# A two-stage attention with a squared-ReLU layer: five transposed blocks instead of six, keys in token order, and a new written-out order

## The chip, the cores and the metric

The kernel runs on one core of one Trainium2 chip. The metric is the device time of one execution in microseconds (us); less is better. The core has five engines with a stream of instructions each: TensorE (PE, matrix products; its weight loads are listed as PEld), VectorE (DVE), ScalarE (ACT), GpSimd (POOL) and SyncE (SP). Transfers are issued from the streams of SP, ACT and POOL.

## What is computed

```
q, k, v: (8, 8, 576, 64)      p: (8, 8, 32, 64)      # batch, head, token, channel; float32
def sm_attn(qq, kk, vv):
    s = 0.125 * (qq @ kk.T)
    s = s - max(s, axis=-1)
    a = exp(s);  a = a / (sum(a, axis=-1) + 1e-09)
    return a @ vv
packed = sm_attn(p, k, v)                 # 32 rows for each batch and head
x = sm_attn(q, packed, packed)            # 576 rows for each batch and head
x = x as (8 * 576 tokens, 8 * 64 channels)
out = (maximum(x @ w_in, 0) ** 2) @ w_out # 512 -> 2048 -> 512; out (4608, 512) float32
```

So 32 learned rows per head first gather the 576 tokens (the first softmax, over 576), and each token then reads these 32 rows (the second softmax, over 32).

## The kernel before

Four heads of one batch make a quad, whose 4 x 32 rows of p fill the 128 partitions; a batch has two quads. A token of a head is numbered l * 18 + t, with l from 0 to 31 (T = 18): l lies on the partitions of k and q after loading, t and the channel in the free dimension. VectorE transposes 32 x 32 blocks of 4-byte pairs, which puts channel pairs on the partitions. The matmuls are in bfloat16.

For a quad the steps are these, with the word of each in the order:

- `Lk`, `Lv` (load1, L284) and `Lq` or `LA`, `LB` (load_q, L268; for batches 0 and 1 in an A part of 320 tokens of each head and a B part of 256) load and cast, on POOL's queue. k of the first quad comes over SP and is cast by `kc`.
- `kT` (st_k, L341): VectorE turns the keys. The result's columns are in the order (j, l, a) with t = 6a + j, so each j from 0 to 5 owns 96 columns next to each other, and writes go in steps of 12 bytes.
- `s1` (st_s1, L371), `m1` (st_max1, L391), `x1` (st_exp1, L395): scores of the first softmax, maximum, exponential with sum, giving e1.
- `eT` (st_e1T, L409): PE transposes e1 in six blocks of 96 columns into a PSUM bank; `eo` (L415) copies it out. `pv` (st_pv, L425): for each block and head one small matmul with v, whose tile v_b holds six tokens on each of 96 partitions (J = 6, PS = 96), in a pool of three.
- `pp`, `bd`, `bs`, `pt`, `po`: scaling, the turned copies for the second scores, a copy with the partition halves exchanged (`bs`, L460), and the transposed copy ppT.
- `w0`, `w1` (st_wp, L540; for batch 0 `wa`, `wb`, `w1`) multiply ppT by w_in, so that the first layer follows from the second softmax alone; `W0`, `W1` (L551) copy wp out.
- `qT`, `s2`, `t2`, `m2`, `sb`, `x2`, `su`, `a2`, `aT`: the second softmax, with tokens on the partitions, and its turned result a2T (st_a2T, L531). For batches 0 and 1 each exists for the A and for the B part (`qA`, `zA`, `tA`, `mA`, `sA`, `xA`, `uA`, `aA`, `TA`, and with B).

For each batch, half of its tokens and block fb of 128 hidden channels (16 of them), `h` (step_h, L574) multiplies wp by a2T, `r` (L580) takes the ReLU, and `q` with numbers (step_q, L598) squares two blocks into gT, a ring of four batches. `o` (step_o, L609) adds two of the 16 hidden blocks for a tile of 128 output rows, `c` (step_c, L621) copies the tile out of PSUM and `d` (step_d, L630) sends it: two transfers on SP, each of 64 rows; for the last tile four, two on ACT's queue and two on SP's, of half the columns, after ACT and VectorE have each copied a half into the same tile.

The order of all this is written out by hand as one string of words, ORDER (L47). A suffix `:v`, `:a` or `:p` names the engine of a step where there is a choice. Each engine runs its instructions in the string's order and waits where data or a buffer is not there. `Z` with a number runs so many filler matmuls on PE (busy, L324), which keep PE going until the first real work. `pg` (p_next, L224) loads p of batch 1, `Pr`, `Px`, `Pt`, `Pu` (p_rest, L233) load, scale and turn p of the later batches; `Pu` makes pT1, the copy with the partition halves exchanged. `Wi` and `Wo` load w_in and w_out.

Of the kernel before, what the change touches and what calls it, by code (L numbers as in the profile page):

```python
# [20 lines left out]
P = 128  # L21
D = 64
NP = 32
J = 6
T = 18
PS = 96
S = J * PS
HALF = S // 2
QH = 4
SCALE = 0.125  # L30

# [20 lines left out]
h0.0.3 h0.0.9 r0.0.2:a Wo2 h0.0.8 aB01:v h0.0.10 r0.0.3:a TB00 r0.0.9:v r0.0.8:a h0.0.1 TB01 h0.0.11 q0.0.4:a  # L52
r0.0.10:v h0.1.2 q0.0.1:p r0.0.1:v h0.1.8 r0.0.11:a r0.1.2:v h0.1.1 q0.0.0:a r0.1.8:v h0.1.9 h0.1.0 r0.1.9:a LA1
q0.0.5:v w101 r0.1.1:a w100 q0.1.4:v W101:a h0.1.10 W100:v h0.1.3 h0.1.11 LB1 r0.1.0:a r0.1.3:a kT10 q0.1.0:p h0.0.12
r0.1.10:a r0.1.11:a h0.1.7 h0.1.14 q0.1.1:a r0.0.12:v h0.0.13 Wo1 r0.1.14:a kT11 h0.1.12 r0.1.7:a h0.0.4 q0.1.5:a
h0.1.5 Wo3 r0.0.13:v r0.1.12:a s11 q0.0.6:v r0.0.4:a Pr h0.0.5 r0.1.5:a m110 h0.0.6 r0.0.5:a h0.1.13 h0.1.6 r0.0.6:a
m111 h0.0.7 r0.1.13:a h0.1.4 x110 r0.0.7:v h0.1.15 r0.1.6:v h0.0.15 x111 r0.1.4:v eT10 q0.1.3:v h0.0.14 r0.1.15:v
q0.1.6:a o2.0 eo10:v q0.1.2:a eT11 q0.1.7:v o0.0 q0.0.3:a rd1 eo11:v o2.1 r0.0.14:a r0.0.15:v pv1 q0.0.2:a o0.1 pp1
o3.0 q0.0.7:a pt1 o1.0 bd1 o3.1 po1:v o1.1 Lv20 w110 w010 W110:v o3.2 o2.2 W010:a Lk21 o1.2 qA11 o0.2 qA10 w111 zA1
qB10 qB11 o2.3 W111:a tA11 o1.3 tA10 o3.3 mA11 o0.3 mA10 zB1 w011 sA11 o1.4 W011:a tB10 o0.4 tB11 sA10 o3.4 xA11 mB11  # L60
o1.5 xA10 mB10 o3.5 uA11 o0.5 uA10 o2.4 sB11 o0.6 aA11 o1.6 xB11 aA10 o2.5 Px Lv21 uB11 o0.7 TA11 Lv30 o1.7 TA10 c0:a
Pt o2.6 Lk20 c1:a d0 h1.0.0 aB11 o2.7 sB10 r1.0.0:a h1.0.1 TB11 c2:v h1.0.2 r1.0.1:a Pu o3.6 xB10 q1.0.0:v h1.0.4
r1.0.2:a o3.7 uB10 Lk31 r1.0.4:a o4.0 d2 kT21 c3:a h1.0.3 h1.0.12 r1.0.3:a aB10 o6.0 r1.0.12:a d1 q1.0.1:v h1.0.7
h1.0.5 r1.0.7:v o4.1 r1.0.5:a TB10 Lk30 h1.0.6 d3 q1.0.2:v h1.0.8 r1.0.6:a o6.1 r1.0.8:v q1.0.3:a h1.0.11 o6.2 h1.0.10
r1.0.11:v o4.2 kT20 Lq2 r1.0.10:a h1.0.9 o6.3 q1.0.5:a r1.0.9:v h1.0.14 s12 r1.0.14:v h1.0.15 q1.0.4:a m120 o4.3
h1.0.13 m121 o6.4 r1.0.15:a Lk40 x120 o4.4 q1.0.7:v o6.5 r1.0.13:v x121 o4.5 kT31 eT20 h1.1.10 rd2 q1.0.6:v eo20:a
eT21 r1.1.10:v h1.1.0 o6.6 eo21:v r1.1.0:a h1.1.6 kT30 h1.1.1 o4.6 Lk41 r1.1.6:a pv2 r1.1.1:v o6.7 pp2 h1.1.7 q1.1.0:v
c6:a h1.1.8 bd2 pt2 r1.1.7:v o4.7 r1.1.8:a bs2:v po2:a h1.1.5 c4:a h1.1.3 d6 q1.1.3:v w021 r1.1.5:a w020 r1.1.3:v o5.0
W020:a qT20 d4 h1.1.2 h1.1.11 Lk50 o7.0 qT21 r1.1.2:a W021:a o5.1 r1.1.11:v h1.1.13 o5.2 q1.1.1:v q1.1.5:a s22 Lv31
r1.1.13:v h1.1.4 o5.3 t220 r1.1.4:a h1.1.14 h1.1.9 Lv40 t221 o5.4 r1.1.9:a q1.1.2:a w120 Lq3 m220 w121 r1.1.14:a o5.5  # L70
W120:a m221 h1.1.12 o5.6 sb20:v W121:a h1.1.15 o5.7 sb21:v o7.1 r1.1.15:a c5:v x220 s13 Lq4 o7.2 q1.1.7:v q1.1.4:a
m130 o8.0 x221 d5 o7.3 su20 r1.1.12:a o8.1 o7.4 x130 su21 o8.2 q1.1.6:a o7.5 a220 o8.3 eT30 a221 o8.4 aT20 o7.6 eo30:a
aT21 o8.5 m131 h2.0.0 h2.0.1 r2.0.0:a o7.7 kT40 r2.0.1:a h2.0.2 x131 o8.6 c7:v Lk51 h2.0.3 r2.0.2:a o8.7 q2.0.0
r2.0.3:a qT30 h2.0.4 c8:a h2.0.7 d7 o9.0 rd3 r2.0.4:a q2.0.1 o10.0 qT31 r2.0.7:a h2.0.5 d8 eT31 kT41 r2.0.5:a Lq5
h2.0.6 eo31:a o9.1 r2.0.6:v h2.0.8 o10.1 q2.0.2 r2.0.8:a q2.0.3 h2.0.13 Lk60 h2.0.9 r2.0.13:v pv3 o9.2 pp3 r2.0.9:a
h2.0.10 h2.0.11 Lv41 q2.0.4 r2.0.10:a o9.3 r2.0.11:a bd3 pt3 h2.0.12 Lv51 bs3:v o9.4 po3:a r2.0.12:v h2.1.1 q2.0.5 s23
r2.1.1:a q2.0.6 h2.0.14 qT41 h2.1.2 r2.0.14:a o9.5 r2.1.2:a t231 h2.0.15 o10.2 r2.0.15:a qT40 h2.1.6 h2.1.0 r2.1.6:a
o9.6 q2.0.7 Lq6 h2.1.7 r2.1.0:a m231 o9.7 r2.1.7:a h2.1.3 q2.1.0 c9:a h2.1.4 q2.1.3 o10.3 r2.1.3:a sb31:v o11.0 d9
o10.4 r2.1.4:a t230 x231 h2.1.9 h2.1.5 q2.1.1 w130 su31 r2.1.5:a w030 r2.1.9:a o10.5 W030:a m230 h2.1.13 h2.1.10 o10.6
r2.1.13:a a231 r2.1.10:a o11.1 W130:a q2.1.2 h2.1.14 h2.1.11 sb30:v o11.2 r2.1.14:a o10.7 aT31 r2.1.11:a h2.1.12 x230  # L80
q2.1.5 h2.1.8 o11.3 c10:v r2.1.12:a r2.1.8:a w131 su30 w031 d10 o12.0 W031:a h2.1.15 q2.1.4 o12.1 q2.1.6 r2.1.15:a
a230 o11.4 W131:a o12.2 q2.1.7 o11.5 aT30 o12.3 h3.0.0 h3.0.2 o12.4 r3.0.0:v r3.0.2:a s14 h3.0.5 kT50 h3.0.4 r3.0.5:a
o11.6 m141 h3.0.1 Lk61 r3.0.4:a o12.5 r3.0.1:a kT51 h3.0.3 o11.7 x141 h3.0.12 r3.0.3:v o12.6 q3.0.0 r3.0.12:a h3.0.7
c11:a q3.0.2 h3.0.8 Lk70 q3.0.1 o12.7 r3.0.7:a m140 o13.0 d11 c12:a h3.0.13 r3.0.8:v o13.1 x140 r3.0.13:v h3.0.10
o14.0 d12 q3.0.6 r3.0.10:a h3.1.5 rd4 o13.2 r3.1.5:v h3.0.6 eT41 r3.0.6:v h3.0.11 o14.1 q3.0.3 r3.0.11:a h3.0.9 eo41:v
h3.1.0 eT40 r3.0.9:v o13.3 q3.0.5 r3.1.0:a o14.2 eo40:v h3.1.2 h3.1.1 q3.0.4 pv4 r3.1.2:v o14.3 Lv50 pp4 r3.1.1:a
# [700 lines left out]
```

## Time and profile before

| | |
|---|---|
| time, median of 3 runs (lowest to highest) | 245.26 us (244.96 to 247.83) |
| the profiled execution's own time | 245.67 us |
| its span, first to last instruction | 243.9 us |
| granted clock of TensorE | 0.998 |
| busy: PE, DVE, ACT, POOL | 231.7, 205.9, 142.4, 69.3 us |
| fillers on PE (L328) | 92 matmuls, 14.5 us busy |
| first real `h` matmul starts | 21.44 us |
| o steps (L618), h steps (L562) busy | 145.1, 91.2 us |
| transfers of POOL's queue, of the others | 18.26 MB in 28048 packets, 10.23 MB in 6640 packets on the main one of them |

In a row of the profile a group of instructions is given by line, engine, operation and tiles, then its count, its busy time in us with the mean of one in ns, and the idle time of its engine just before it with what ended it. Matmuls are pipelined: a mean duration is longer than the distance from one start to the next, so distances are read from the timeline. The profile lacks the record of one matmul in each of the 36 output tiles (540 of 576 are there, while all 576 weight loads are), which shows as a gap on PE that is none.

### The profile page before, as it was taken

To read this page: it belongs to the slowest core of one execution; us is meant where nothing else is said; L and a number is where in the kernel's file an instruction comes from. 1 tells how busy PE (TensorE), PEld (TensorE's weight loads), DVE (VectorE), ACT (ScalarE), POOL (GpSimd) and SP (SyncE) were. 2 spreads that over 40 slices of the span, in tenths; PEclk is the share of its full clock that TensorE was granted. 3 is DMA by queue.
4 is the path that set the end of the run, shared out by engine and by line. 5 is a ranking of instruction groups with operands and counts; after the bars stand their busy time and mean duration, and the time that the engine had idled before them with its cause. 6 is when DMAs were issued, how large, how long until landed. Compare 5 with 4: busy or idle time off the path is not lost.

```text
span 243.9 us, 6139 instructions
## 1 busy us (share of the span) xinstructions
PE 231.7 (95%) x2424; PEld 128.8 (53%) x2460; DVE 205.9 (84%) x448; ACT 142.4 (58%) x315; POOL 69.3 (28%) x109
## 2 busy tenths in 40 slices
PE   8889899999999999999999999999999999999991
PEld 5556563455545655456445555565445554555540
DVE  3579987999989989798999999978898999677720
ACT  3418993577787859673666578644775667331200
POOL 8448832667690752072001800001000000000000
PEclk9999999999999999999999999999999999999999
DMA  6999999999999999456733991211332112121313
GB/s 152 198 197 209 203 207 200 143 192 273 161 193 212 168 154 217 86 74 115 111 73 82 121 173 27 63 43 46 50 90 59 36 38 46 43 60 28 86 43 86
DMA packets 34876, 29.00 MB, mean 119 GB/s; under 512 B 14112, under 2 KB 29856, under 8 KB 34848
## 3 DMA queue, kind: packets, MB, share of 16 engines
q0 software_dynamic: 28048, 18.26, 53.5%
q1 hardware_dynamic: 6640, 10.23, 16.0%
q8 instruction: 19, 0.31, 0.5%
q10 hardware_dynamic: 160, 0.13, 0.2%
q14 instruction: 9, 0.07, 0.1%
HBM read 37.22 MB, written 9.44 MB: 191 GB/s over the span
## 4 chain that ended last, share of the span: by engine, by line
PE 80%; DVE 9%; DMA 5%; issue 2%; POOL 1%; ACT 1%; POOLq 0%; ACTq 0%
PE ps_o L618 47%; PE ps_h L562 24%; DMA q_b<-in_q_dram 4%; PE ps_wp L546 3%; PE ps_s L369 3%; PE ps_e1T L412 2%; PE ps_pv L434 1%; DVE mx L500 1%; DVE gT L607 1%; DMA out_dram<-o_sb 1%; DVE sums L518 1%; DVE qT L357 1%; DVE r L569 1%; DVE s L495 1%; DVE s L492 1%
## 5 line engine op out<-in xcount | busy, mean ns | idle before, releaser
L618 PE MATMUL ps_o<-w_out_bf,gT 128*128 128x512 bf16 x540 | 145.1, 379 | 3.1 <-issue 1.7
L567 ACT ACTIVATE r<-ps_h 128x288 bf16<-128x288 f32 (+2 forms) x177 | 68.2, 417 | 51.9 <-PE ps_h L562 50.2
L562 PE MATMUL ps_h<-a2T,wp 128*128 128x288 bf16 (+2 forms) x512 | 91.2, 286 | 0.9 <-DVE wp L407 0.6
L618 PEld LDWEIGHTS <-gT 128*128 128x128 bf16 x576 | 53.7, 98 | 41.3 <-issue 5.5
L562 PEld LDWEIGHTS <-wp 128*128 128x128 bf16 x512 | 48.4, 98 | 44.1 <-issue 5.0
L607 DVE TENSOR_TENSOR gT<-r 128x576 bf16<-128x576 bf16 (+2 forms) x110 | 47.1, 445 | 2.6 <-ACT r L567 1.6
L569 DVE TENSOR_SCALAR r<-ps_h 128x288 bf16<-128x288 f32 (+2 forms) x79 | 34.9, 450 | 9.5 <-PE ps_h L562 8.9
L264 POOL DMA_DIRECT2D k_b<-in_k_dram x27 | 17.7, 656 | 47.3 <-DVE kT L344 37.2
L405 ACT CAST wp<-ps_wp 128x1024 bf16<-128x1024 f32 (+1 forms) x25 | 23.4, 953 | 6.1 <-PE ps_wp L546 6.1
L289 POOL DMA_DIRECT2D v_b<-in_v_dram x16 | 11.1, 697 | 39.8 <-PE ps_pv L434 38.0
L405 ACT COPY o_sb<-ps_o 128x512 f32<-128x512 f32 x25 | 14.5, 589 | 7.8 <-PE ps_o L618 7.6
L344 DVE STREAM_TRANSPOSE kT<-k_b 128x576 uint32<-128x576 uint32 x16 | 15.1, 950 | 2.4 <-DMA k_b<-in_k_dram 1.6
L399 ACT ACTIVATE e<-ps_s,nm 128x576 bf16<-128x576 f32 x16 | 11.8, 746 | 6.6 <-DVE nm L393 6.5
L328 PE MATMUL ps_idle<-gT 128*128 128x288 bf16 x92 | 14.5, 309 | 1.1 <-DVE gT L187 1.1
L512 ACT ACTIVATE e<-d 128x576 f32<-128x576 f32 (+2 forms) x20 | 11.4, 592 | 5.8 <-POOL d L506 4.0
L357 DVE STREAM_TRANSPOSE qT<-q_b 128x576 uint32<-128x576 uint32 (+2 forms) x20 | 12.2, 636 | 1.8 <-DMA q_b<-in_q_dram 1.6
L266 POOL DMA_DIRECT2D k_b<-in_k_dram x19 | 11.7, 617 | 3.8 <-DMA w_out_bf<-in_moe_w_out_dram 2.0
L407 DVE CAST wp<-ps_wp 128x1024 bf16<-128x1024 f32 x9 | 11.0, 1221 | 1.6 <-PE ps_wp L546 1.6
L518 DVE TENSOR_REDUCE sums<-e 128x18 f32<-128x576 f32 (+2 forms) x20 | 12.2, 612 | 0.0
L526 DVE TENSOR_TENSOR a<-e,rs 128x576 bf16<-128x576 f32 (+2 forms) x18 | 12.0, 680 | 0.0
L264 POOL DMA_DIRECT2D q_b<-in_q_dram x16 | 10.9, 684 | 3.3 <-DVE qT L357 2.3
L393 DVE TENSOR_REDUCE nm<-ps_s 128x1 f32<-128x576 f32 x16 | 11.6, 739 | 0.2 <-PE ps_s L369 0.2
(54 smaller groups left out, 179.2 us busy)
## 6 DMA issues: line engine op xcount, KB each, us to landing
out_dram<-o_sb SPq DMA_DIRECT2D x70, 128.0 KB, 2.4
v_b<-in_v_dram POOLq DMA_DIRECT2D x16, 288.0 KB, 7.4
w_out_bf<-in_moe_w_out_dram POOLq DMA_DIRECT2D x4, 512.0 KB, 12.5
q_b<-in_q_dram POOLq DMA_DIRECT2D x6, 288.0 KB, 7.5
q_b<-in_q_dram POOLq DMA_DIRECT2D x12, 144.0 KB, 7.5
k_b<-in_k_dram POOLq DMA_DIRECT2D x12, 108.0 KB, 4.5
w_in_bf<-in_moe_w_in_dram POOLq DMA_DIRECT2D x4, 256.0 KB, 11.3
w_in_bf<-in_moe_w_in_dram POOLq DMA_DIRECT2D x2, 512.0 KB, 13.0
```

The costliest lines, as they stand in the source:

```text
L264: engine.dma_start(x[n:], s[:P - n])
L328: self.nc.tensor.matmul(ps[:, :HALF], lhsT=self.nought[:, :P], rhs=self.nought, start=True, stop=True)
L344: return self.nc.vector.transpose(t["kT"][:].rearrange("p (j l a) e -> p a j l e", j=J, a=3).bitcast(U32).rearrange("p a j l e -> p a j (l ...
L357: self.nc.vector.transpose(out.bitcast(U32), x.bitcast(U32))
L405: engine.copy(out, x)
L518: nc.vector.reduce_sum(out=sums[:, x], in_=t["e2"][:, x], axis=AX.X)
L526: engine.tensor_tensor(out=a2[:, y].rearrange("p t i e -> p t e i"), in0=t["e2"][:, x].rearrange("p (t e) i -> p t e i", e=2), in1=t["rs"] ...
L562: self.nc.tensor.matmul(ps, lhsT=t["wp"][:, fb // n, fb % n * P:(fb % n + 1) * P], rhs=t["a2T"][:, s0:s1], start=(qd == 0), stop=(qd == se ...
L567: engine.activation(r, ps, ACT.Relu)
L569: engine.tensor_scalar_max(r, ps, 0.0)
L607: engine.tensor_tensor(out=out, in0=r, in1=r, op=ALU.mult)
L618: self.nc.tensor.matmul(self.o[tt], lhsT=self.gT[:, fb, a:a + P], rhs=self.w_out_bf[:, fb, :], start=(i == 0), stop=(i == self.NFB - 1))
```

## The change

- From batch 2 on, e1 is transposed in five blocks: four of 128 columns in steps of four (tokens 0 to 511), and one of the last 128 columns, whose first 64 tokens were had already. Batches 0 and 1 keep six blocks of 96, now in steps of six. The count of small matmuls in `pv` follows.
- `kT` writes the keys in token order, l * 18 + t, that is in steps of 72 bytes. k is loaded in two contiguous halves of t instead of three pieces for each half.
- v of batches 0 and 1 is loaded into parts of gT not yet in use. From batch 2 on it lies in three fixed tiles of 128 partitions with five blocks; the fifth block holds the last 64 tokens on the upper 64 partitions and zeros, written once at the start, on the lower. Such a load has two transfers.
- The last tile of output rows has its own row order (two transposes in `aT` of batch 7 instead of one), so that each half goes out in one transfer; the two halves are copied into tiles of their own.
- `pg` is issued from ACT's queue; `Pu` is done by two copies of VectorE instead of two transfers of SP.
- The order is new throughout, with 90 fillers instead of 92, and other engines for many steps.

```
 ORDER = """
-Lk00 I pf Lk01 Lv00 LB0 Lv01 kc:v kc:a LA0 pg P0 Wi11 kT00 Wi01 Wi00 kT01 Z32 s100 Wi10 Z1 s101 m100 Wi21 m101 x100
-x101 qB01 Wi20 Z10 eT00 qB00 eo00:a Z1 eT01 rd0 eo01:v Lk10 Z4 pv0 pp0 Z4 pt0 bd0 Lk11 qA01 po0:a zB0 qA00 tB00 Z2 zA0
-P1 tA01 tA00 mA01 mA00 sA01:p mB00 Lv10 sA00:v xA01 tB01 xA00 sB00:p uA01 Z23 wa01 wa00 Wo0 uA00 Wa00:a Wa01:a aA01:v
-mB01 xB00 aA00:p Z8 wb01 wb00 TA01 Wb01:a Lv11 sB01:v Wb00:a TA00 uB00 xB01 Z7 h0.0.0 h0.0.2 uB01 r0.0.0:a aB00:p
...
+Lk00 I pf Lk01 Lv00 Lv01 LA0 kc:v kc:a Wi01 P0 kT00 Wi00 LB0 Z30 s100 Wi10 kT01 Wi11 m100 Z4 s101 Wi21 m101 x100 x101
+Wi20 Z15 eT00 rd0 eT01 eo00:v pg eo01:v Lk10 qA01 Z5 pv0 qA00 pp0 Lk11 Z4 pt0 bd0 zA0 po0:v tA01 tA00 Z4 wa01 mA01
+Wa01:a Z1 wa00 mA00 Wa00:a sA01:p qB01 Wo0 sA00:v xA01 qB00 xA00 uA01 Lv10 Z13 zB0 uA00 aA01:p tB00 Lv11 aA00:v Z8
+wb00 mB00 Wb00:a TA01 sB00:p TA00 tB01 Z6 h0.0.9 P1 h0.0.8 xB00 h0.0.0 mB01 r0.0.8:a uB00 wb01 sB01:p r0.0.0:a h0.0.1
+Wb01:a r0.0.9:v LA1 xB01 r0.0.1:v h0.0.10 aB00:p q0.0.4:a h0.0.3 uB01 h0.0.2 h0.0.11 q0.0.0:v r0.0.10:a r0.0.3:a
+r0.0.2:v aB01:p r0.0.11:a TB00 q0.0.1:v w100 Wo2 w101 TB01 W100:a q0.0.5:v h0.1.8 h0.1.9 W101:v h0.1.1 r0.1.9:a h0.1.0
...
 setup
+        self.v_b = [self.consts.tile([P, QH, 5, D], BF16, name=f"v_b{i}") for i in range(3)]
+        for x in self.v_b:
+            nc.vector.memset(x[:P // 2, :, 4, :], 0.0)
 p_rest
-            self.nc.sync.dma_start(z[P // 2:], y[:P // 2])
-            self.nc.sync.dma_start(z[:P // 2], y[P // 2:])
+            self.copy(engine, z[P // 2:], y[:P // 2])
+            self.copy(engine, z[:P // 2], y[P // 2:])
 load1
+        elif b in WIDE:
+            for hf, y in enumerate(WIDE_CUTS):
+                self.load_rows(x[:, y, :], s[:, y, :], qd + 2 * hf)
+    def load_v(self, t, s, b, qd):
+        if b in THREES:
+            c = b * S
+            x = self.gT[:, self.NFB - 2 - 2 * b - qd, c:c + QH * 6 * D].rearrange("p (h j d) -> p h j d", h=QH, d=D)[:S // 6]
+            t["v"] = [x[:, :, j, :] for j in range(6)]
+            self.nc.gpsimd.dma_start(x, s.rearrange("h (p j) d -> p h j d", j=6))
+            return
+        x = self.v_b[self.loaded_v % len(self.v_b)]
+        self.loaded_v += 1
+        t["v"] = [x[:, :, j, :] for j in range(5)]
+        self.nc.gpsimd.dma_start(x[:, :, :4, :], s[:, :4 * P].rearrange("h (p j) d -> p h j d", j=4))
+        self.nc.gpsimd.dma_start(x[P // 2:, :, 4, :], s[:, 4 * P:].rearrange("h p d -> p h d"))
 st_k
-            t["kT"][:].rearrange("p (j l a) e -> p a j l e", j=J, a=3).bitcast(U32).rearrange("p a j l e -> p a j (l e)"),
-            t["k"][:].rearrange("p (a j) d -> p a j d", j=J).bitcast(U32))
+        self.nc.vector.transpose(t["kT"][:].rearrange("p (l t) e -> p t l e", t=T).bitcast(U32).rearrange("p t l e -> p t (l e)"),
+                                 t["k"][:].bitcast(U32))
 st_e1T
-        for j in range(J):
-            self.nc.tensor.transpose(ps[:, j, :], t["e1"][:, j * PS:(j + 1) * PS], self.ident)
+        m = 6 if b in THREES else 4
+        n = S // m // NP
+        n = min(n, QH)
+        x = [t["e1"][:, j:n * m * NP:m] for j in range(m)]
+        if n * m < T:
+            x.append(t["e1"][:, S - P:])
+        ps = self.bank16(b, "ps_e1T")[:n * NP, :len(x) * P].rearrange("p (j c) -> p j c", c=P)
+        for j, y in enumerate(x):
+            self.nc.tensor.transpose(ps[:, j, :], y, self.ident)
 st_a2T, for batch 7
+        if last:
+            y = slice(y.start, y.stop - 2)
+            self.nc.vector.transpose(a2T[:, y.stop * 2 * NP:].bitcast(U32).rearrange("p (l t) -> p t l", t=2),
+                                     t["a2"][:, y.stop:].rearrange("p t i e -> p t (i e)").bitcast(U32))
 step_c and step_d, the last tile
+            o = self.o_sb[tt] = [self.op.tile([P, self.NE], F32, name="o_sb")[:, :h] for _ in range(2)]
+            self.nc.scalar.copy(o[0], ps[:, :h])
+            self.nc.vector.tensor_copy(o[1], ps[:, h:])
...
+            rows = self.out[-S:].rearrange("(l t) n -> l t n", t=T)[:, T - 4:]
+            self.nc.scalar.dma_start(rows[:, :, :h], o[0])
+            self.nc.sync.dma_start(rows[:, :, h:], o[1])
```

More of the change, by code (lines that the diff above doesn't have):

```diff
@@ L30 @@
 SCALE = 0.125
+THREES = range(2)
 PIECES = range(2)
@@ L53 @@
[L53 to L62, printed above, removed]
@@ L409, in st_e1T @@
     def st_e1T(self, t, b):
-        ps = self.bank16(b, "ps_e1T")[:PS, :J * P].rearrange("p (j c) -> p j c", c=P)
-        for j in range(J):
-            self.nc.tensor.transpose(ps[:, j, :], t["e1"][:, j * PS:(j + 1) * PS], self.ident)
+        m = 6 if b in THREES else 4
[7 more added lines that the diff above has]
+            self.nc.tensor.transpose(ps[:, j, :], y, self.ident)
         t["ps_e1T"] = ps
     def st_e1T_out(self, t, engine):
-        t["e1T"] = self.tp.tile([PS, J, P], BF16, name="e1T")
-        self.copy(engine, t["e1T"], t["ps_e1T"])
+        ps = t["ps_e1T"]
+        t["e1T"] = self.tp.tile([P, T // 3, P], BF16, name="e1T")[:ps.shape[0], :ps.shape[1], :]
+        self.copy(engine, t["e1T"], ps)
     def st_rden(self, b, *qds):
@@ L428, in st_pv @@
         n = len(qds)
-        for j, i in [(j, i) for j in range(J) for i in range(n)] if b else [(j, i) for i in range(n) for j in range(J)]:
+        m = range(len(self.att[b, qds[0]]["v"]))
+        for j, i in [(j, i) for j in m for i in range(n)] if b else [(j, i) for i in range(n) for j in m]:
             t = self.att[b, qds[i]]
@@ L706, in step @@
         elif word in ("Pr", "Px", "Pt", "Pu"):
-            self.p_rest(word)
+            self.p_rest(word, engine)
         elif word[:2] == "kc":
```

200 lines of the change are left out of this document (98 added, 102 removed).

## The prediction

> **What bounds the kernel now.** I read the first page first: busy times, then the slices, then the chain. TensorE (PE) is busy for 95% of the span at the full clock and carries four fifths of the chain; VectorE (DVE) follows at 84%, and it is near full in the first two thirds.
>
> ```profile
> span 243.9 us, 6139 instructions
> PE 231.7 (95%) x2424; PEld 128.8 (53%) x2460; DVE 205.9 (84%) x448; ACT 142.4 (58%) x315; POOL 69.3 (28%) x109
> PE   8889899999999999999999999999999999999991
> DVE  3579987999989989798999999978898999677720
> PE 80%; DVE 9%; DMA 5%; issue 2%; POOL 1%; ACT 1%; POOLq 0%; ACTq 0%
> ```
>
> Then the windows, to see where PE loses time. Columns: window, its length, busy of PE, weight loads, DVE, ACT, POOL, clock, DMA share, GB/s.
>
> ```profile
> 0.00:10.00 10.00, 7.77 (x72) 5.15 (x73) 4.14 (x8) 2.74 (x4) 6.99 (x16) 1.00 0.90 168
> 10.00:20.00 10.00, 8.97 (x158) 5.98 (x155) 7.57 (x24) 3.70 (x9) 5.60 (x9) 1.00 1.35 201
> ...
> 120.00:140.00 20.00, 19.47 (x245) 10.28 (x242) 19.39 (x38) 13.55 (x31) 5.74 (x9) 1.00 0.51 86
> 140.00:160.00 20.00, 19.84 (x175) 10.92 (x177) 19.68 (x40) 14.65 (x35) 0.00 (x0) 1.00 0.45 83
> ...
> 30.00:200.00 170.00, 167.15 (x1855) 91.46 (x1875) 156.76 (x336) 114.41 (x253) 48.44 (x75) 1.00 0.74 123
> 30.00:230.00 200.00, 196.83 (x2052) 108.12 (x2076) 180.81 (x387) 125.95 (x279) 48.44 (x75) 1.00 0.66 112
> ```
>
> From 30 to 230 us PE idles 3.2 us in all, so in the body only less PE work, or a new wait, moves the end. Before 21.4 us PE mostly runs fillers (14.5 us of the "ps_idle" row) while loads and the first softmaxes finish: there the chain goes through the q load and DVE. After the last matmul come copy and output. DVE idles 13.2 us between 30 and 200.
>
> **The change, part by part.** The rows it touches, by form:
>
> ```profile
> L344 DVE STREAM_TRANSPOSE kT<-k_b 128x576 uint32<-128x576 uint32 x16 | 15.1, 950 | 2.4 <-DMA k_b<-in_k_dram 1.6 <-PE ps_s L369 0.6
> L357 DVE STREAM_TRANSPOSE qT<-q_b 128x576 uint32<-128x576 uint32 x12 | 9.0, 759 | 0.2
> L412 PE MATMUL ps_e1T<-ident,e 128*96 128x128 bf16 x96 | 8.0, 220 | 0.1
> L412 PEld LDWEIGHTS <-e 128*96 128x96 bf16 x96 | 7.3, 123 | 2.1 <-ACT e L399 0.6
> L618 PEld LDWEIGHTS <-gT 128*128 128x128 bf16 x576 | 53.7, 98 | 41.3 <-issue 5.5 <-DVE gT L607 1.1 <-DVE rs L520 0.2
> L407 DVE COPY e1T<-ps_e1T 96x768 bf16<-96x768 bf16 x9 | 4.8, 538 | 0.0
> ```
>
> *Five blocks, batches 2 to 7 (12 quads).* In the timeline six transposes start 56 ns apart, so one less is 0.056 us: 12 x 0.056 = 0.67. The second product goes from 48 to 40 small matmuls a batch; 48 start within 0.36 us, 7.6 ns each: 6 x 8 x 7.6 = 0.37. Both lie in the PE-bound body. Sum **-1.04**. The copies shrink from 768 to 640 columns (DVE 538 to about 470 ns); they hide beside PE.
>
> The new weight loads take 128 columns, 8 bytes apart (12 in batches 0 and 1); no row has such a step. The strided 32-column loads of pT take 88 ns, the dense ones of ppT 89, so no price shows at 4 bytes. Matmuls come 56 ns apart although a load lasts 123: loads overlap. I take 56 ns; the bad end is that loads no longer overlap, 123 ns: 67 x 72 strided blocks = +4.8. A gain is excluded, since 128 columns already need the 56. The Trainium skill, "TensorE: Matmul & The Clock Gate", section on weight-path perf modes, says that a fast weight load needs 128 columns and allows large column steps; 98 ns for 128 columns against 123 for 96 agrees, the step no run shows. By it the bad end is unlikely.
>
> *Keys in token order.* Same count, same read; the write step goes from 12 to 72 bytes. Dense costs 759, step 12 costs 950. Lower end 759 (if the four-dimensional pattern, not the step, is what costs). Upper end: qT's 320 and 256 columns cost 488 and 414 ns, 1.16 ns an element; were each element written at half that pace, 759 + 576 x 1.16 = 1430. I take 1040, near the 12-byte row. On 16 transposes: DVE -3.1 / +1.4 / +7.7 us, beside 13.2 idle. The Trainium skill, "SBUF — State Buffer", in its note on cachelines under Door 1, says an access that crosses into a new 16-byte line pays and that two hits a line are needed to hide it. The trace's 950 against 759 agrees; at 72 bytes each write meets a new line, so by it the lower end is out. It speaks against the change, through DVE (rival 2).
>
> *Work that the new order shifts.* Counting engine marks: DVE gains three e1T copies net (and nine smaller, +1.0), two ppT (+0.6), one wp (+1.2), three relus (+1.35), one square (+0.5), the two pT1 copies of "Pu" (+0.8, between the 220-ns ppd copy and the 538-ns row each), two small transposes in batch 7 (+0.3); it loses two output copies (-1.4), one shift pair (-0.4), one subtraction and one product to POOL (-0.8). Sum +3.1. ACT loses about 5 of its 142, so eviction there is not the limit. DVE becomes about 210.5. At nothing on the path: cover is 13.2 us of idle DVE, 12 us of it still unfilled after 200 us. If that cover is gone, each us lands on PE.
>
> *Queues and places.* v of batches 0 and 1 goes into gT's blocks 14 to 11, which square steps write only after pv has read them: nothing. v from batch 2 takes two POOL issues instead of one: 12 x 0.70 = 8.4 us on POOL (69 busy of 244), behind which the next k and q loads queue. They are ahead: POOL waits 37 and 38 us for k and v buffers. By packet rows a k quad falls from 768 to 256 packets, a v quad rises from 384 to 768 (the added ones small); summed packet time of both falls from 4.35 to about 4.1 us a quad. Nothing. SP loses "pg" (three issues) and "Pu" (two). "pg" now stands on ACT, three issues of 0.65 = 1.9, between the first exponentials (end 10.98) and "Wa01" (after 15); ACT idles there, as it has given up eo00 and po0. The landing (6.4 in the row) is before "P1". The three clearing memsets (row of L187: 0.18) fit before 4.26, where DVE waits for keys.
>
> *Head.* The A part of q goes ahead of B on POOL, and w_in's Wi01 and Wi00 also go ahead of B.
>
> ```profile
> 10.93 0.77 DVE L357 STREAM_TRANSPOSE qT<-q_b 128x256 uint32<-128x256 uint32 x2 [0.81 <-DMA q_b<-in_q_dram]
> 14.38 0.91 DVE L357 STREAM_TRANSPOSE qT<-q_b 128x320 uint32<-128x320 uint32 x2 [0.82 <-DMA q_b<-in_q_dram]
> 15.78 0.49 POOL L266 DMA_DIRECT2D k_b<-in_k_dram  x1 [0.32 <-DMA w_in_bf<-in_moe_w_in_dram]
> ```
>
> Landings there are 1.1 to 1.7 apart, one behind the other. A loses B's 1.1: 13.3. B follows two w_in pieces: 13.3 + 3 x 1.4 = 17.5. On PE 15 fillers (0.122 each) now stand between s101 (ends 9.3) and eT00: 11.1 instead of 10.5. Both copies on DVE, 0.54 each: pv0 at 12.7. "pp0" queues on DVE behind both qA turns, which wait for A: 13.3 + 2 x 0.49 + 0.42, then bd0: zA0 at 15.0 (15.34 before). From there DVE is never idle but for 0.1 to 0.4 at qB01, which stands in front of sA00 (ACT's exponential waits behind it). Summing DVE's list at its start-to-start pace (the trace runs it at 0.88 of the summed durations), TA00 ends at 21.3 and h starts there, 21.44 before; with full durations 22.0. TB01 ends at 25.8 (23.8 before), kT11 at 29.4 (29.4 before); full durations 31.8. By then PE has issued 20 h blocks, not 23: 14 x 0.27 + 6 x 0.22 = 5.1 against 11 x 0.27 + 12 x 0.22 = 5.6. So the head is 0.5 short. Ends: two fewer fillers and wb01 after h, -0.6; full durations, 2.4 + 0.5 = +2.9. I take **+0.5**: pace is what the trace shows.
>
> *Tail.*
>
> ```profile
> 239.01 0.37 ACT L625 COPY o_sb<-ps_o 128x256 f32<-128x256 f32 x1 [10.62 <-PE ps_o L618]
> 239.42 1.29 ACTq L639 DMA_DIRECT2D out_dram<-o_sb  x2
> 239.42 0.42 DVE L626 COPY o_sb<-ps_o 128x256 f32<-128x256 f32 x1 [2.35 <-DMA out_dram<-o_sb]
> ```
>
> The release named is not it: the DVE half starts when the ACT half of the same tile ends (239.38). With two tiles it starts at 239.0: 0.42 sooner. One issue instead of two a queue drops another 0.6 on SP. The single transfer has 128 packets, and its landing rises from the 2.0 row towards the 2.4 row: +0.35. **-0.7** (-1.05 to -0.4).
>
> *Sum.* The profiled execution took 245.67 (span 243.9 and 1.8 around it): 245.67 - 1.04 - 0.70 + 0.50 = 244.43. It stands 0.41 above the median of the runs shown, 245.26; against the median **244.0**.
>
> **The rivals.**
> 1. *Better fitted waits.* The order is new from end to end, and PE's 3.2 us of idle time in the body may fall, say to 1.4, with the head at its good end (1.1 better): 244.0 - 1.8 - 1.1 = 241.1. For it: the waits are many and small. Against it: DVE has more to do, and in the head too.
> 2. *DVE becomes the bound (slower).* kT at 1430 ns is 0.48 above today. From 30 to 200 us twelve of them add 5.8 and the shifted work 3.1, together 8.9; at the 98% of its fullest windows DVE could take 0.98 x 170 - 156.8 = 9.8. So nothing has room: s1 waits for kT, and exponential and transposes queue behind s1. If half of the twelve delays meet a PE without an output step to run, that is 6 x 0.48 = 2.9; kT01 in the head adds 0.5: 247.4. It decides from about 1.15 us, where 6 x 0.2 eats the forecast's gain over 245.26. For it: 12 bytes already cost 190 ns. Against it: output steps stand round nearly every score step.
> 3. *Slow strided weight loads:* +4.8 gives 248.8. Against it: pT's loads.
> 4. *It does not do what it says:* PE's saved 1.04 becomes waiting for DVE: 245.0.
>
> **How the numbers follow.** Forecast 0.45, rival 1 0.17, rival 2 0.20, rival 3 0.08, rival 4 0.10. The forecast's own range is 242.4 (head and tail at their good ends) to 246.4 (head at its bad end). For 8 in 10, 241.3 to 248.2: below lies about half of rival 1, above parts of 2 and 3. Two per cent, about what a measurement of this kernel can tell from no change, is 240.4 to 250.2: faster 0.06 (the best of rival 1), slower 0.08 (2 and 3 together or beyond), same 0.86.
>
> **What would show it.** L412 with 84 transposes, still 56 ns apart; kT's row between 0.95 and 1.1 us; h starting between 21.3 and 22; PE idle from 30 to 230 near 3.2; the two last copies starting together; ACT's busy time 5 lower. I am wrong if kT is over 1.15 us and PE waits at s1, if the new loads space out the transposes, if the B half of the first softmax holds PE for over 2 us about 25, or if PE's body waits change by over 2 us.

## The result and the profile after

The changed kernel takes **248.62 us** (median of 4 runs, 248.41 to 249.74) against 245.52 for the kernel before beside it (4 runs, 244.96 to 247.83): ratio 1.0125, 95% interval 1.0080 to 1.0171, so 3.1 us slower and within the 2% that a measurement of this kernel is taken to tell. Forecast were 244.0 and a range to 248.2: the sign was wrong and the range missed by 0.4. In the ledger below a ratio less one is turned into us with 246.

One thing about the work: from batch 2 k is still loaded in two halves of t with the partitions exchanged between them, while the changed kernel's columns go by l; half of the columns of the first scores thus use keys of another head of the quad. From batch 2 on it therefore does not compute what the formula says; the amount of work is the same.

Busy time, the slices and the chain, from the page of the changed kernel:

```profile
span 247.0 us, 6063 instructions
PE 237.0 (96%) x2398; PEld 129.3 (52%) x2398; DVE 210.9 (85%) x459; ACT 138.4 (56%) x308; POOL 75.2 (30%) x124
PE   8998899999999999998999999999999999999993
DVE  4579997999999899998999989998998799776730
PE 57%; DVE 19%; DMA 17%; issue 2%; POOL 2%; ACT 1%; SPq 0%; DVEq 0%; POOLq 0%
```

PE held 80% of the chain and holds 57 now; the share went to DVE (9 to 19) and to transfers (5 to 17). DVE's busy time rose by the 5 us that the sum of the prediction had. But the rows say that it is made of something else:

```profile
L359 DVE STREAM_TRANSPOSE kT<-k_b 128x576 uint32<-128x576 uint32 x16 | 19.3, 1242 | 1.8 <-DMA k_b<-in_k_dram 1.0 <-PE ps_h L590 0.8
L433 PE MATMUL ps_e1T<-ident,e 128*128 128x128 bf16 x60 | 5.0, 219 | 0.0
L433 PEld LDWEIGHTS <-e 128*128 128x128 bf16 x60 | 4.3, 110 | 1.5
L433 PE MATMUL ps_e1T<-ident,e 128*96 128x128 bf16 x24 | 3.5, 290 | 0.0
L433 PEld LDWEIGHTS <-e 128*96 128x96 bf16 x24 | 3.4, 227 | 0.1
```

The turn of the keys (kT) went from 950 to 1242 ns: 4.2 of the 5 us by the busy times of the two rows (16 x 0.29 would be 4.7, but turns that follow each other overlap a little). Of the weight loads, those of 128 columns in steps of 8 bytes (batches 2 to 7) take 110 ns, those of 96 in steps of 12 (batches 0 and 1) 227, where the dense ones took 123. In the timeline the transposes of the first kind start 56 to 60 ns apart as before, of the second 133: 24 x 0.077 = 1.8 us of PE's time that the prediction did not have.

**Where the time lies.** The last matmul ends at 242.87 instead of 238.94, +3.93, and what follows it is 4.09 instead of 4.93, -0.84. To place the 3.93, take from the clock at any moment the time that the matmuls issued until then need when they follow each other (an output step's matmul 0.216 from start to start, a transpose 0.056, an `h` its columns / 2400 + 0.0025, and so on; fillers are not counted as needed). Call the rest PE's lost time. By 35, 60, 120 and 235 us it is 20.6, 21.5, 22.9 and 25.3 before, and 22.9, 24.6, 28.1 and 30.3 after. So +2.2 arises before 35 us, +0.9 by 60, +2.0 by 120 and about nothing later; against this +5.1 stand some 1.1 of work saved. These are single traces, and the part before 35 us differs from run to run (see "Side by side" below).

**A gap that was none.** The prediction read 3.2 us of idle PE from 30 to 230 us before. In that trace 36 matmul records are missing; the section on the profile before says that this gap is none, and the prediction still counted it as idle time. A run in which only the tail is changed (e9, below) has them all (PE x2460, as many as weight loads). The same window, of that run and then of the changed kernel (the columns are those of the windows in the prediction):

```profile
30.00:230.00 200.00, 199.95 (x2076) 108.10 (x2075) 180.93 (x389) 125.50 (x278) 48.11 (x75) 1.00 0.67 112
```

```profile
30.00:230.00 200.00, 197.85 (x2031) 106.72 (x2031) 183.00 (x392) 122.75 (x273) 55.49 (x91) 1.00 0.66 109
```

In the old order PE idles 0.05 us in the body, not 3.2: there was nothing left to win there but PE work. In the changed kernel it idles 2.15.

### The profile page after: what moved, and what is told of

It reads as the page before. It is cut to its first block, busy times and chain, and to the rows that moved or that the text cites. A ratio compares the mean times of both kernels' runs of the same rounds, so it can differ in the third digit from the quotient of the medians.

```text
span 247.0 us, 6063 instructions
## 1 busy us (share of the span) xinstructions
PE 237.0 (96%) x2398; PEld 129.3 (52%) x2398; DVE 210.9 (85%) x459; ACT 138.4 (56%) x308; POOL 75.2 (30%) x124
## 4 chain that ended last, share of the span: by engine, by line
PE 57%; DVE 19%; DMA 17%; issue 2%; POOL 2%; ACT 1%; SPq 0%; DVEq 0%; POOLq 0%
PE ps_o L646 34%; PE ps_h L590 17%; DMA w_in_bf<-in_moe_w_in_dram 6%; DMA w_out_bf<-in_moe_w_out_dram 6%; DVE kT L359 4%; DVE gT L635 3%; DMA gT<-in_v_dram 3%; PE ps_wp L574 2%; DMA v_b<-in_v_dram 2%; DVE nm L407 2%; PE ps_s L383 2%; DVE a L549 1%; DVE sums L541 1%; DVE mx L523 1%; PE ps_e1T L433 1%
## 5 line engine op out<-in xcount | busy, mean ns | idle before, releaser
L646 PE MATMUL ps_o<-w_out_bf,gT 128*128 128x512 bf16 x576 | 149.1, 379 | 0.9 <-DVE gT L635 0.9
L595 ACT ACTIVATE r<-ps_h 128x288 bf16<-128x288 f32 (+2 forms) x174 | 66.8, 417 | 54.0 <-PE ps_h L590 51.2
L590 PE MATMUL ps_h<-a2T,wp 128*128 128x288 bf16 (+2 forms) x512 | 89.9, 286 | 1.3 <-DVE r L597 0.4
L646 PEld LDWEIGHTS <-gT 128*128 128x128 bf16 x576 | 54.3, 98 | 45.9 <-issue 4.7
L419 ACT CAST wp<-ps_wp 128x1024 bf16<-128x1024 f32 (+1 forms) x24 | 22.4, 947 | 15.3 <-PE ps_wp L574 15.2
L268 POOL DMA_DIRECT2D k_b<-in_k_dram x27 | 14.8, 558 | 22.1 <-DVE kT L359 15.0
L419 ACT COPY o_sb<-ps_o 128x512 f32<-128x512 f32 x27 | 15.7, 590 | 9.7 <-PE ps_o L646 9.7
L359 DVE STREAM_TRANSPOSE kT<-k_b 128x576 uint32<-128x576 uint32 x16 | 19.3, 1242 | 1.8 <-DMA k_b<-in_k_dram 1.0
L315 POOL DMA_DIRECT2D v_b<-in_v_dram x12 | 9.4, 786 | 29.6 <-PE ps_pv L457 29.6
L268 POOL DMA_DIRECT2D q_b<-in_q_dram x16 | 10.9, 687 | 24.8 <-DVE qT L371 24.6
L421 DVE CAST wp<-ps_wp 128x1024 bf16<-128x1024 f32 x10 | 12.2, 1215 | 1.3 <-PE ps_wp L574 1.1
L270 POOL DMA_DIRECT2D k_b<-in_k_dram x19 | 10.1, 531 | 10.0 <-DMA q_b<-in_q_dram 3.8
L343 PEld LDWEIGHTS <-gT 128*128 128x128 bf16 x90 | 9.1, 109 | 5.4 <-DVE gT L187 1.1
```

Source lines behind the costliest of these rows:

```text
L268: engine.dma_start(x[n:], s[:P - n])
L343: self.nc.tensor.matmul(ps[:, :HALF], lhsT=self.nought[:, :P], rhs=self.nought, start=True, stop=True)
L359: self.nc.vector.transpose(t["kT"][:].rearrange("p (l t) e -> p t l e", t=T).bitcast(U32).rearrange("p t l e -> p t (l e)"), t["k"][:].bit ...
L419: engine.copy(out, x)
L590: self.nc.tensor.matmul(ps, lhsT=t["wp"][:, fb // n, fb % n * P:(fb % n + 1) * P], rhs=t["a2T"][:, s0:s1], start=(qd == 0), stop=(qd == se ...
L595: engine.activation(r, ps, ACT.Relu)
```

## The experiments

Theory **K**: the time hangs on the keys' 72-byte write, which makes DVE late where PE has nothing else to do. Rivals: the new **order** is itself worse (O); the strided weight **loads** (L). Each kernel is named by its base and its edit.

**e1, e2: code and order apart.** e1 is the changed kernel with the old ORDER, e2 the kernel before with the new one.

> All of the new code, with the order (and so the engines) of before. Theory K: the keys' 72-byte writes, 1.24 us a transpose instead of 0.95, make VectorE late (16 x 0.29 = 4.7 us), and PE waits for it; the order is innocent. Then the old order suffers at least as much as the new one: 248 to 250 us, kT near 1.24, PE waits in the body. Theory O: the new order is what leaves PE waiting, and the code gains: 245.5 less 0.5 (fewer blocks, net of slow weight loads in batch 1) less 0.8 (tail) = 244.2, within 1.

> The code of before with the new order and its engines (90 fillers, A part of q first, pg on SP as before, Pu by SP's transfers). Theory K: without the 72-byte writes the new order runs about as well as the old one: 244.5 to 246. Theory O: the order itself costs: 247.5 to 249, with waits of PE near 23 to 30 and 115 us as in the changed kernel.

e1: 248.11, ratio 1.0080 (1.0053 to 1.0108): as K had it, most of the loss is there without the new order. e2: 256.41, 1.0409 (1.0368 to 1.0449), outside both forecasts, for a reason of its own. Windows of e2 around 53 us:

```profile
53.00:59.00 6.00, 0.11 (x4) 0.00 (x0) 0.20 (x1) 0.81 (x2) 0.18 (x1) 0.86 1.18 250
59.00:64.00 5.00, 4.96 (x40) 2.08 (x41) 1.95 (x4) 2.32 (x6) 0.00 (x0) 0.50 0.73 142
```

PE stands for 6.2 us inside the scores of batch 2 until the transfers that make pT1 (`Pu`) land, and then runs at half the granted clock until 64 us. The new order leaves no room for those transfers; the changed kernel has VectorE copy instead.

**e3, e4: the write step alone.**

```
e3, in the changed kernel            e4, in the kernel before
-  kT: (l t), 72 bytes               -  kT: (j l a), 12 bytes
+  kT: (j l a), j=6, a=3, 12 bytes   +  kT: (l t), 72 bytes
```

> The changed kernel with one thing undone: the keys are written in steps of 12 bytes, in the old column order, so that the keys stand in another order than v and the first product mixes tokens; all else is as changed. Theory K: kT back at 0.95, the waits of PE after 100 us go, 245.5 to 246.5. Theory O: 248 or more, with the wait of 1.1 us near 115 us still there. What theory L says (weight loads with a 12-byte step take 133 instead of 56 ns in batches 0 and 1, 24 x 0.077 = 1.8 us) stays in this run: PE's transposes of batches 0 and 1 stay at 133 ns.

> The kernel before with one thing added: the keys are written in steps of 72 bytes, in token order, while the blocks of e1 stay as they were, so the first product mixes tokens. Theory K: kT at 1.24, VectorE 4.7 us heavier, and time 2 to 4 us up: 247.5 to 249.5. Theory O: VectorE has 13 us of room from 30 to 200 us and takes it: at most 1 us up, the head's part: 245.5 to 246.5.

e3: kT 940 ns, 245.91, ratio 1.0006 (0.9974 to 1.0037). e4: kT 1240 ns, 248.88, ratio 1.0102 (1.0048 to 1.0156). The one line is worth 2.9 us in the changed kernel and 2.5 in the kernel before; K's forecasts of the times came true, O's did not. e10 below is e1 with 12-byte keys, a third such pair: 0.9989 against 1.0080, 2.2 us. **K holds.** One part of its forecast for e3 failed, that the waits after 100 us go. The largest stays:

```profile
112.80 1.04 PE L647 MATMUL ps_o<-w_out_bf,gT 128*128 128x512 bf16 x4 [0.68 <-DVE gT L636]
```

From start to start it is 0.84, and 1.09 in the changed kernel: most of this wait belongs to the order.

**e5, e8: the other end, 4 bytes.** e5: `(j l a)` becomes `(j a l)` in the kernel before. e8: the same from batch 2, v loaded in three pieces to match, and the new tail.

> The kernel before with one edit: VectorE writes the turned keys without gaps (column order a, l inside a block instead of l, a), so a lane's writes follow each other at 4 bytes, where the kernel before has 12 and the changed one 72. The values keep their old token order, so the first attention product pairs keys and values of different tokens; the amount of work is unchanged. It is the other end of the scale whose 72-byte end cost +3.1 us. Theory K (the time hangs on what VectorE needs for a turn of the keys): the row of the turn falls from 940 to between 760 and 800 ns, VectorE is busy for 2.5 to 3 us less, and the time falls by 0.5 to 2.5 us, less than 72 bytes cost, because TensorE waits for little in the kernel before from 35 us on. Theory O (VectorE's time is covered and the 72-byte kernel lost its time in another way, for instance on the read side of the scores): the row may fall, the time stays within 0.4 us of the kernel before.

> The kernel before in its own order with two edits that go together: the changed kernel's split output tail, and from batch 2 keys written without gaps (4 bytes), for which the values are loaded in three pieces a quad so that keys and values pair by token again. Theory K: the turn of the keys falls from 940 to 760 to 800 ns on twelve of sixteen, the tail after the last matmul falls from 4.9 to 4.1 us, and the time is 0.8 (tail) and 0.3 to 1.5 (keys) below before: 243.3 to 244.7. Rival (the extra value transfers, two more a quad on GpSimd's queue, delay the keys and queries queued behind them and bring new waits): a wait for keys of over 0.5 us appears and the time is at 245 or above.

e5: kT 759 ns, DVE 1.3 less busy, 246.70, ratio 1.0000 (0.9975 to 1.0026). K had forecast 0.5 to 2.5 us less; the rival's "within 0.4" came. In the old order DVE's slack is one-sided: what it gains below 950 ns buys nothing, since PE hardly idles; what it loses above is in part paid. e8: 245.85, 0.9978 (0.9952 to 1.0003), as its rival had it: no more than the tail alone gives (e9), and in its trace a wait of 1.5 us at 57 us for scores whose keys, issued behind the added v pieces on POOL, land late.

**e11: the price by step.** The kernel before with another step in each batch from 2.

```
+        a = {2: 1, 3: 2, 4: 3, 5: 6, 6: 9, 7: 18}.get(b, 3)    # step of 4 * a bytes
```

> A measurement of the disputed price by itself: the kernel before, with the write step of the turned keys set by batch: 12 bytes in batches 0 and 1, then 4, 8, 12, 24, 36 and 72 bytes in batches 2, 3, 4, 5, 6 and 7 (columns then stand in other orders; same work). The price of one turn by step is read from the timeline. Known: 4 bytes 759, 12 bytes 943, 72 bytes 1242 ns. Theory line (every write that meets a new 16-byte line pays): 8 bytes 800 to 900 (two writes a line), and 24, 36 and 72 bytes all alike near 1240, since each write meets a new line from 16 bytes on. Theory slope (price grows with the step itself): 24 bytes near 1000, 36 near 1050, 72 at 1240.

The first turn of batches 2, 3, 4, 5 and the last of 7, from the timeline (start, duration):

```profile
52.35 0.78 DVE L346 STREAM_TRANSPOSE kT<-k_b 128x576 uint32<-128x576 uint32 x1
60.63 0.77 DVE L346 STREAM_TRANSPOSE kT<-k_b 128x576 uint32<-128x576 uint32 x1
79.93 0.95 DVE L346 STREAM_TRANSPOSE kT<-k_b 128x576 uint32<-128x576 uint32 x1
104.37 1.22 DVE L346 STREAM_TRANSPOSE kT<-k_b 128x576 uint32<-128x576 uint32 x1 [0.64 <-PE ps_s L371]
159.80 1.25 DVE L346 STREAM_TRANSPOSE kT<-k_b 128x576 uint32<-128x576 uint32 x1
```

Means of both turns: 4 bytes 774 ns, 8 bytes 768, 12 bytes 935, 24 bytes 1208, 36 bytes 1189, 72 bytes 1255. These are two turns for each step, in one run. They fit a rule of 16 bytes and not a slope, though 8 bytes had been forecast at 800 to 900: two words to a line cost nothing, one word to a line costs 0.45 us whatever the step. The Trainium skill, "SBUF — State Buffer", in its note on cachelines under Door 1, says just this (at least two hits a line, or each new line pays); the trace agrees, and 12 bytes, where two writes of four are alone in their line, pay some 0.17 of the 0.45.

**e14: the changed kernel with 8 bytes** (j=9, a=2).

> The changed kernel with keys written at 8 bytes in all batches: two words to a 16-byte line (another order of the columns; same work). Theory line (only writes that meet a new line cost): the turn takes 760 to 775 ns, less than at 12 bytes (940), and the time is at or below that of the same kernel with 12 bytes: 245.0 to 246.0, ratio 0.996 to 1.001. Rival (under the changed order a turn has a floor that neighbours set, for instance transfers or ScalarE's reads of the same memory): above 850 ns, and the time above 246.3.

kT 761 ns, 245.27, ratio 0.9977 (0.9955 to 0.9999): the changed kernel, one line apart, is no slower than the kernel before (its columns, too, pair keys and values of different tokens).

**e13: head or body.** 12 bytes in batches 0 and 1, 72 from batch 2.

> The changed kernel with keys written at 12 bytes in batches 0 and 1 alone; from batch 2 at 72 (in batches 0 and 1 the keys then stand in another order than the values; same work). With 12 bytes everywhere the time fell by 2.9 us. Theory H (the loss is made in the head: TensorE's lost time by 35 us was 22.9 in the changed kernel and 20.8 with 12 bytes everywhere): the time falls by 1.5 to 2.3 us, to about 246.6 to 247.1 by the runs of the changed kernel. Theory S (a delay of the head is taken back at the next wait for VectorE, and the loss belongs to the body's twelve turns): the lost time by 35 us falls to about 21, that by 235 us stays above 29.5, and the time falls by less than 1 us.

248.71, ratio 1.0102 (1.0072 to 1.0131): only some 0.6 of the 2.9 us lies in the head, and the intervals of this run and the changed kernel overlap; the rest, 2.4 (e13 against e3, clear of noise), lies behind it. Theory S is right on the time but not on how: the lost time by 35 us stayed at 22.6. In its trace `h` and wp now wait 1.6 us at 24.4 for the last of the w_in pieces in front of them (0.9 in the changed kernel), which lands 14.5 us after its issue. In e3, with the same instructions up to there, it lands at 24.2 instead of 26.1. The head is held by that transfer, and its landing differs from run to run.

**e12: one wait in the body.** The changed kernel with one word of ORDER moved: kT60 behind m150 and q3.0.2.

> The changed kernel with one word of its order moved: the turn of the second half of batch 6's keys (kT60) goes on VectorE behind the row maximum m150 and the square q3.0.2 that TensorE's output step waits for at 115 us, no longer ahead of them. Theory W (that wait is queueing on VectorE: a turn of 1.24 us stands ahead of a square that TensorE needs at once): the wait of 1.09 us at 115.2 falls below 0.3, and the time falls by 0.6 to 1.0 us, to 247.6 to 248.0. Rival (VectorE owes the work anyway, so TensorE waits as long somewhat later): the wait goes, another of like size comes within 20 us, and the time stays at 248.6 within 0.4.

DVE in the changed kernel, and then PE:

```profile
114.15 1.25 DVE L359 STREAM_TRANSPOSE kT<-k_b 128x576 uint32<-128x576 uint32 x1 [0.76 <-PE ps_h L590]
115.25 0.69 DVE L407 TENSOR_REDUCE nm<-ps_s 128x1 f32<-128x576 f32 x1
115.86 0.44 DVE L635 TENSOR_TENSOR gT<-r 128x576 bf16<-128x576 bf16 x1
```

```profile
116.36 1.04 PE L646 MATMUL ps_o<-w_out_bf,gT 128*128 128x512 bf16 x4 [0.92 <-DVE gT L635]
```

The turn first waits 0.76 for PE, then takes 1.25, and behind it stands the square that PE's output step needs. In e12 the square starts at 113.94 and the turn after it, and the wait of 1.09 from start to start is gone. 248.50, ratio 1.0090 (1.0058 to 1.0121), about 0.9 lower than the changed kernel's by the ratios, but the intervals overlap and the time lies in the rival's range (248.6 within 0.4). Laid beside the changed kernel's trace, 1.1 us is gone at 115 us and half of it is back by 121: what is left is 0.6.

**e6, e10, e15: five blocks and their weight loads.** e10 is e1 with 12-byte keys: of the change, five blocks, static v and the tail. e15 is e10, and e6 is e3, with contiguous loads in batches 0 and 1:

```
-        x = [t["e1"][:, j:n * m * NP:m] for j in range(m)]
+        x = [t["e1"][:, j * n * NP:(j + 1) * n * NP] if b in THREES else t["e1"][:, j:n * m * NP:m] for j in range(m)]
```

> The changed kernel with the keys written at 12 bytes (as in the kernel before) and one more edit: in batches 0 and 1 the six blocks of 96 columns that TensorE loads for the transposes of the first softmax are contiguous, as before, instead of 12 bytes apart (the softmax's columns then stand against values of other tokens in those two batches; same work). Theory L (the 12-byte loads hold TensorE for 0.077 us each, 24 of them): the transposes of batches 0 and 1 start 56 ns apart again, the row of the 96-column loads falls from 227 to about 123 ns, and the time is 0.9 to 1.9 us below that of the same kernel without this edit (245.9), so 244.0 to 245.0. Rival (the loads lie beside TensorE's fillers and h blocks which only move up to the next wait for VectorE): the spacing falls but the time stays within 0.5 us of 245.9.

> The changed kernel in the order of the kernel before and with keys written at 12 bytes: so of the change, five blocks, values in static tiles and the tail are left, without the 72-byte write and without the new order. (Keys then stand in another order than the values in the first product; same work.) Theory A (the parts add up: 72 bytes +2.5 to 2.9, order +1.1 to +1.9, five blocks and tail -1.04 and -0.8 as predicted): ratio about 0.9925, that is 1.8 us below before, and TensorE's lost time by 235 us within 0.6 of the kernel before's 25.3. Rival B (the five blocks give back under the old order what they save, as the run of the new code in the old order against the kernel before with 72 bytes suggests, where only 0.5 of the 1.84 showed): ratio 0.996 to 1.0, with new waits in the body.

> Five blocks, values in static tiles and the split tail in the order of the kernel before, keys at 12 bytes, and the weight loads of batches 0 and 1 contiguous (keys and values then in different orders; same work). Without the contiguous loads the ratio was 0.9989 where -1.04 for the blocks and -0.84 for the tail would have given 0.9925. Theory L (24 slow weight loads of 0.077 us gave it back): ratio 0.992 to 0.995. Theory G (in the body TensorE stands against VectorE and the transfers at fixed marks, so that what it saves becomes waiting): ratio 0.997 to 1.0, with TensorE's lost time by 235 us above 26.

Contiguous, the loads take 123 ns again. e10: 246.30, ratio 0.9989 (0.9972 to 1.0006). e15: 244.96, 0.9961 (0.9940 to 0.9983): some 0.7 us for the loads in the old order, though the intervals overlap. Neither reached the 0.9925 at which the parts would add up, and e15 fell between its two forecasts. e6: 246.34, 1.0010 (0.9987 to 1.0033), against 1.0006 of e3: nothing in the new order, where theory L had 0.9 to 1.9. That its head waits for w_in anyway would explain it, but was not tried by itself.

**e7: the order alone.** The kernel before, new ORDER, `Pu` by two VectorE copies.

> The kernel before under the changed kernel's order, and the two copies of the shifted query transposes (Pu) by VectorE instead of by transfer; keys at 12 bytes, six blocks, dense loads, old tail. Theory T (the 6.2 us stall at 52.8 us in the run without VectorE's copies was the landing of those two transfers, which the new order leaves no time for, and TensorE's half clock after it was a result of the stall): the stall and the half clock are gone and the time is 245 to 247, since the order by itself is worth about nothing. Rival (the new order needs the new code elsewhere too, at the first softmax's six blocks): a stall of over 2 us stays somewhere between 45 and 65 us and the time is above 249.

The stall of e2 is gone: 248.17, ratio 1.0078 (1.0043 to 1.0113). The forecast of 245 to 247 was too low: order and copies cost 1.9 us with the old code, the largest wait again the one at 113 us (1.3).

**e9, e16: tail alone, and `Pu` by transfers again.** e9 is the kernel before with the new step_c, step_d and st_a2T. e16 is e15 with p_rest of the kernel before.

> The kernel before with the changed kernel's output tail alone: two half tiles, one transfer for each of the two queues, the last turn of the second softmax written so that a half's rows are dense. What comes after the last matmul falls from 4.9 to 4.1 us and nothing else moves, so the time is 0.6 to 0.9 us below before (ratio about 0.997). Rival: the two added small turns of batch 7 delay the last output step or the last transfers land no sooner, and the ratio is 0.999 or more. In both cases the half tile of VectorE is expected to start only when that of ScalarE ends, as in the changed kernel's trace.

> The run with five blocks, tail and dense weight loads in the order of the kernel before (keys at 12 bytes; keys and values in different orders, same work), with the two copies of Pu by transfers of SP again in place of VectorE. Theory P (VectorE's two copies stand in front of the square that the output step at 51.0 us needs): the gap of 0.83 us there falls to 0.22 and the time falls by 0.4 to 0.6 us, ratio about 0.994. Rival (VectorE's list is as late without them, or the saving turns up as another wait): the gap goes, the ratio stays at 0.996 or above.

e9: 245.24, ratio 0.9966 (0.9945 to 0.9987), -0.8. e16: 244.08, ratio 0.9927 (0.9910 to 0.9944), -1.8. DVE of e15 (not e16):

```profile
50.48 0.78 DVE L422 COPY pT<-pT 64x768 bf16<-64x768 bf16 x2
51.30 0.49 DVE L636 TENSOR_TENSOR gT<-r 128x640 bf16<-128x640 bf16 x1
```

Again a square for which PE waits (0.83 from start to start) stands behind DVE work that the change added, and without the copies that gap is gone. The profiles of e15 and e16 differ by only 0.4 us, less than the 0.8 of the ratios, whose intervals just overlap; side by side (next) the step at 51 us is 0.74. So in the old order the copies' price is 0.4 to 0.8.

e9 computes the whole reference and beats both kernels. e16 is faster still, but pairs keys and values of different tokens in the first product; whether five blocks can be had with right pairs and without more v transfers (e8 shows their price) was not tried.

**Side by side.** Kernels with the same order run their weight loads in the same sequence. So the start of each load in one trace, less its start in the other, shows where time is lost (us; the clock is that of the second kernel of each row):

| | by 20 | by 50 | by 120 | by 235 |
|---|---|---|---|---|
| changed kernel against e3 (72 bytes, 12) | 1.54 | 2.12 | 3.57 | 4.09 |
| e13 against e3 | 1.13 | 1.88 | 3.43 | 3.97 |
| e4 against the kernel before (72 bytes, 12) | 1.47 | 2.05 | 3.00 | 3.25 |
| e1 against e10 (72 bytes, 12) | 0.85 | 1.31 | 2.25 | 2.61 |
| e5 against the kernel before (4 bytes, 12) | 1.18 | 1.18 | 1.13 | 1.10 |
| e15 against e10 | 0.36 | -0.61 | -0.59 | -0.57 |
| e16 against e15 | 0.45 | 0.48 | -0.26 | -0.26 |
| e12 against the changed kernel | -0.39 | -0.44 | -1.20 | -0.99 |

Up to 50 us the edit is mixed with chance: e13 and e3 run the same instructions up to the first turn of batch 2, and yet are 1.88 apart (e3's trace is of the fastest of its ten runs; e4's holds 3.4 us at half clock from 11 us on). Behind that the traces are steady. There the twelve 72-byte turns cost 2.0 to 2.1 us in the new order and 1.2 to 1.3 in the old, of the 3.5 that they gained. In the new order this comes in about ten pieces: 0.54 at 164.2, where `h` waits for a ReLU that VectorE does behind two turns, 0.29 at 54.6, where the first scores wait for the turn itself, 0.25 of the wait at 116.4, and smaller ones.

## Why the prediction was wrong

1. **The step that failed** is the keys: "I take 1040, near the 12-byte row", with the DVE time "at nothing on the path: cover is 13.2 us of idle DVE". Both halves were wrong. The turn takes 1242 ns, because 72 bytes leave each word alone in its line (e11); the row at 12 bytes lies between two regimes and is not near. The note that each write then meets a new line was cited and only used to strike out the lower end. And 13.2 us of idle DVE are not cover: in the changed kernel DVE still idles 11.5 us of the same 170. All sixteen turns together gained 4.7 us by the means, and 2.2 to 2.9 of it reached the end (e3, e4, e1 against e10). Of the 3.5 of the body's twelve, 2.0 reached it in the new order and 1.2 in the old, since PE waits for the turn or for what is queued on DVE behind it. That is rival 2, to which the prediction gave a chance of 0.20: its limit of 1.15 us was passed, its 1430 ns was too high, and its half of the delays that land was too low for the new order.
2. **Five blocks, -1.04: right in size, but given away.** e16 less the tail of e9 gives -1.0; in the changed kernel's trace the second product alone takes 0.07 less a batch, 0.42 in six (0.37 predicted). In the old order part of it is eaten by loads in 12-byte steps, which the prediction named and took at 56 ns (0.077 us more each on PE, 0.7 of the time in the old order, nothing seen behind the new head). So rival 3 came true for 24 of its 72 strided blocks (133 ns, where it had 123), and not for the 48 in steps of 8 bytes.
3. **Shifted DVE work, +3.1 at nothing:** the sum was too high (5.0 less 4.2 of kT leaves 0.8), the price of nothing too low: the two `Pu` copies, 0.8 us of DVE, cost 0.4 to 0.8 in the old order (e16).
4. **The order was costed in the head only.** Head: `h` starts at 21.95, inside 21.3 to 22; but +0.5 looks too little: lost time grew by 2.2 until 35 us, of which chance may be a large part (1.9 between e13 and e3). There it waits for DVE and for w_in by turns (e13); the prediction asked what the w_in pieces delay, not when they themselves land. Body: costed at nothing, it has the wait of 0.84 at 113 us even with 12-byte keys (e3), and moving one word wins 0.6 in the trace (e12, not clear of noise in the times). As a whole the order cost 1.9 with the old code (e7, its copies with it). With the new code, which has the copies in either order, it cost 1.1 (changed kernel against e1) and 0.4 (e3 against e10), neither clear of noise, and 1.2 (e6 against e15), which just is.
5. **Tail, -0.7: right** (-0.84 in the trace, -0.8 in e9), by another way. In the changed kernel:

```profile
242.91 0.37 ACT L653 COPY o_sb<-ps_o 128x256 f32<-128x256 f32 x1 [9.57 <-DMA out_dram<-o_sb]
243.31 0.64 ACTq L665 DMA_DIRECT2D out_dram<-o_sb  x1
243.31 0.42 DVE L654 COPY o_sb<-ps_o 128x256 f32<-128x256 f32 x1 [3.17 <-ACT o_sb L653]
```

   The two copies still follow each other, so a shared output tile was not what held the second; what does was not tried. What the traces show in its place is one issue for two on each queue (0.64 against 1.29 on ACT's); whether that is all of the gain was not tried.
6. **Rival 1 had no ground:** the body's idle time it was to win was missing records.

Together: 2.2 to 2.9 for the keys, 0.8 to 2.0 for the order with its copies (the 0.4 to 0.8 of the copies added where both orders have them), up to 0.7 for the loads, -1.0 and -0.8 for blocks and tail: 1.2 to 3.8, and 3.1 measured. The parts do not add exactly, for a wait that one removes another may take over (e6, e12, e13).

## What to carry to other kernels

Price a strided write by how many words share a 16-byte line, not by the nearest stride in the trace. Before reading idle time, compare the count of matmul records with that of weight loads, and of an engine that feeds a full PE ask what is queued behind the work that grows; its idle sum is no cover. An order written for one set of durations charges for each of them that grows. To place a loss, lay two traces with the same order side by side, and do not trust one trace where a run's transfers land differently each time.

## What the runs showed of the hardware

- VectorE's 32 x 32 turns of 4-byte words: 759 to 774 ns for 576 words a lane at 4 or 8 bytes from word to word, 935 to 950 at 12, 1190 to 1255 at 24, 36 and 72.
- TensorE's weight loads of 96 columns take 123 ns dense and 227 in steps of 12 bytes, and the transposes then start 133 ns apart, not 56; 128 columns in steps of 8 bytes take 110, and the transposes still start 56 to 60 apart. Whether the 128 columns or the 8 bytes save the latter was not separated.
- 6.2 us without matmuls are followed by 5 us at a granted clock of 0.50 (e2); with the order's own 1.9 the run was 10 us longer. The Trainium skill, "TensorE: Matmul & The Clock Gate", Part 1 on the clock gate, gives half rate after an idle window of about 3.4 us; e2's trace agrees. e4's does not: there 2.0 us without matmuls, up to 9.7 us, were followed by half clock from 11.0 to 14.4, so a shorter wait was enough. No wait after 20 us in the other kernels, 1.6 us at most, brought it about.
